# Gain vector by TensorE, remainder rows in strided DMAs, and an earlier second k-by-v product in a fused attention and mixer kernel

## The chip, the cores and the metric

The kernel runs on one core of a Trainium2 chip. The metric is the device time of one execution in microseconds. Before the change the median of three runs was 773.2 us (772.67 to 773.29). Where a single execution is taken apart, the numbers come from the profiled one: 772.69 us, of which the profile's span covers 770.6 us from the first to the last recorded instruction. Times inside the kernel are given from the span's start.

## The reference, cut to what matters

Eight batches, eight heads, 576 tokens, 64 elements to a head. Attention has no softmax: per head it forms `k`-transposed times `v` over the 576 tokens, multiplies `q` with that, divides each row by its root mean square and multiplies by the gain vector `g_norm` (64 numbers, the same for every token and head). The result goes through a mixer over tokens and then one over channels.

```python
kv  = einsum('bhsd,bhse->bhde', k, v)
out = einsum('bhsd,bhde->bhse', q, kv)
x   = out / sqrt(mean(out*out, -1) + 1e-6) * g_norm      # (B,H,S,D) -> (B,S,512)
h   = maximum(x.transpose(0,2,1) @ w_tok1, 0) @ w_tok2   # tokens: 576 -> 256 -> 576
u   = x + h.transpose(0,2,1)
out = u + maximum(u @ w_ch1, 0) @ w_ch2                  # channels: 512 -> 1536 -> 512
```

The four weights arrive as 64-bit floats. The kernel fetches them as pairs of 32-bit words and turns them into 32-bit floats itself.

## The kernel before, in words

**Tiling.** A batch's 576 tokens are split in 512 and a remainder of 64 (`LO` and `HF`, line 61). `k` and `v` of one batch lie in a tile of 128 partitions by five slots by 512 columns (lines 107 and 108): slots 0 to 3 hold the first 512 tokens, four to a partition, and slot 4 holds the 64 remainder rows in partitions 0 to 63. The other half of slot 4 is zeroed once (line 1285). There are two such pairs of tiles, so batch b uses pair b % 2.

**Loading.** `load(b)` (line 140) issues four DMAs: the 1 MB body of `k`, its 128 KB remainder (64 rows of 2 KB, line 148), and the same for `v`. For batch 0 `k` goes through SP's queue and `v` through ACT's; afterwards all go through SP's. `load_q(b)` (line 150) fetches `q`, already transposed, as `qT`. At the start SP issues, in this order, `load(0)`'s k part, `qT` of batch 0, two blocks of the first token weight (`raw`), `load(1)`, `qT` of batch 1, two `q` remainders and the rest of that weight (lines 1275 to 1283). ACT issues `v` of batch 0 and then `g_sb` (line 1294): the 64 gains, copied into all 128 partitions by a DMA whose source repeats the same 256 bytes 128 times.

The framework gives the DMAs of SP and ACT eight completion semaphores in turn, in program order. A DMA that comes ninth waits, on its issuing engine, for the landing of the one that had its semaphore before.

**Steps and their order.** The order of the work is written out by hand as strings of step names (`start`, `middle`, `steady`, `last`), which `play` (line 1256) executes one after the other; each engine runs its own instructions in that order and waits only on data. In the first list the names mean:

- `jN`: N products of the identity with itself, whose result nobody reads (`keep_warm`, line 1333); they keep TensorE busy while data is on its way.
- `kvSH`, `eSH`: k by v for batch S of the pair, half H of the heads (40 matmuls on TensorE, line 371); eviction of the result from PSUM (line 385; by DVE for batch 0 of the first pair, by ACT for batch 1).
- `aCT`: `q` by kv for token group C, tile T (`attend_tile`, line 394); `g`, `q`, `t`, `m`, `r`, `i`, then `d` or `s`: gain times the product (line 451, the reader of `g_sb`), squares, sums, mean, root, inverse, and scaling of the rows by DVE or ACT.
- `hSTJ`: one term of the first token product, batch S, half T of the 256 outputs, token tile J (`tok1`, line 539). It needs x of tile J, that is attention's result, and the weight.
- `wNK`: step K of decoding weight block N. `lS`, `lqS`, `lrS`: the loads of the next pair.

So the first product with a token weight (`h000`) needs the whole chain batch 0's `k`, `v` and `qT`, kv, attention, statistics, scaling and a decoded weight. From then on TensorE has token products, k by v and attention of following batches to alternate between, later the channel products, in which it spends most of the time.

PSUM is used through three pools; the pool `h` of four banks (line 97) serves the products nobody reads, the token products and later the residual sums.

Of the kernel before, what the change touches and what calls it, by code (L numbers as in the profile page):

```python
# [11 lines left out]
F32 = mybir.dt.float32  # L12
# [8 lines left out]
def kernel(  # L21
# [32 lines left out]
    nc = tc.nc  # L54
    P = 128
    B, S, DM = k.shape
    D = g_norm.shape[0]
    H = DM // D
    DTOK = moe_w_tok1.shape[1]
    DCH = moe_w_ch1.shape[1]  # L60
    J, JJ, HF = 4, 5, 64
    LO = P * J
    assert D == 64 and DM == 512 and S == LO + HF and B % 2 == 0
    NC, NF, NTOK = DM // P, DCH // P, DTOK // P
# [13 lines left out]
    def pool(name, bufs, side="left", stack=ctx, **kw):  # L78
        return stack.enter_context(tc.tile_pool(name=name, bufs=bufs, side=side,
                                                reuse_waits="tile", **kw))  # L80
# [9 lines left out]
    inp = pool("inp", 1, "left", left)  # L90
# [5 lines left out]
    ps = {n: pool(f"ps_{n}", b, "left", psums, space=bass.MemoryType.PSUM)  # L96
          for n, b in (("o", 2), ("kv", 2), ("h", 4))}

    ident = inp.tile([P, P], F32, name="ident")
    g_sb = inp.tile([P, 1, D], F32, name="g_sb")  # L100
    w_tok1 = [tokw.tile([P, 2, DTOK], F32, name=f"w_tok1{i}") for i in range(J // 2)]
    w_tok1r = tokw.tile([P, DTOK], F32, name="w_tok1r")
    w_tok2 = tokw.tile([P, NTOK, S], F32, name="w_tok2")
# [10 lines left out]
    def do(f, *a, **kw):  # L114
        return lambda: f(*a, **kw)
# [4 lines left out]
    keep = tc.keep_in_program_order  # L120

    def dma(o, i, engine=nc.sync):
        keep(engine.dma_start(o, i))  # L123
# [7 lines left out]
    def copy(o, a):  # L131
        keep(nc.scalar.copy(o, a))  # L132

    def matmul(*a, **kw):
        keep(nc.tensor.matmul(*a, **kw))  # L135
# [4 lines left out]
    def load(b):  # L140

        if b >= B:
            return

        queues = (nc.sync, nc.sync if b else nc.scalar)
        for dst, t, e in zip((k_in[b % 2], v_in[b % 2]), (k, v), queues):
            dma(dst[:, :J], t[b, :LO].rearrange("(p j) e -> p j e", j=J), e)
            dma(dst[:HF, J], t[b, LO:], e)

    def load_q(b):  # L150
        if b < B:
# [107 lines left out]
    def t_sums(b):  # L259

        def step(o, x, y):
            return lambda: tensor_add(b(o), b(x), b(y), ALU.subtract)

        return [step(5, 7, 1), step(6, 3, 5), step(7, 3, 7), step(4, 2, 6)]
# [96 lines left out]
    def attention(pair, groups):  # L361
# [154 lines left out]
        for s in range(2):  # L516
            for h in range(2):
                steps |= {f"kv{s}{h}": do(kv, s, h), f"e{s}{h}": do(evict, s, h),
                          f"l{s}": do(load, 2 * pair + 2 + s)}
            steps |= {f"lq{s}": do(load_q, 2 * pair + 2 + s), f"lr{s}": do(load_q_rest, 2 * pair + 2 + s)}  # L520
# [75 lines left out]


    xg, xt, uT = {}, {}, {}
    Q = 32
    NQ = T // Q  # L600

    def units(g):
        return ((0,), (1, 2), (3, 4), (5, B), (6, 7))[g] if g < NG else (NU, NU)

    def fetch_x(g):
# [4 lines left out]
        else:  # L610
            xg[g] = late["xg"].tile([P, 2 * NQ, 2, Q], F32, name="xg")
            for b in range(NC):
                dma(xg[g][ds(b * Q, Q)].rearrange("p n l j -> p n (l j)"),
                    u_rows(units(g)[0])[:, ds(DH + b * HF, HF)].rearrange("(n i) e -> i n e", i=Q))

# [14 lines left out]
    def put_blocks(u, half, y):  # L630
        t = blocks_dram[u, half] = dram.tile([NC, Q, NC, 2 * P], F32, name=f"blocks{u}{half}")
        for a in range(NC):
            dma(t[:, :, a].rearrange("b i x -> i b x"),
                y[ds(a * Q, Q)].rearrange("p b o n t -> p b (o n t)"))

# [620 lines left out]
    def play(lines, after={}, **stages):  # L1256

        for name in " ".join(lines).split():  # L1260
            if name.isdigit():
                for _ in range(int(name)):
                    next(stages["rounding"], lambda: None)()
            elif name[0] == "-":
                stages["before"][name[1:]]()
            else:
                next(stages[s][name] for s in ("attention", "mixing", "more")
                     if name in stages.get(s, ()))()
# [4 lines left out]
    channel = ([get_ch1(c, f) for f in range(2) for c in range(NC)]  # L1273
               + [get_ch2(f) for f in range(NF // 2)])
    load(0)
    load_q(0)
    for block in tok1[:2]:
        block[0]()
    load(1)
    load_q(1)  # L1280
    load_q_rest(0)
# [5 lines left out]
    for t in zeroed:  # L1287
# [3 lines left out]
    keep(nc.vector.memset(root, 1.0))  # L1291
    keep(nc.scalar.activation(root, root, AF.Sqrt))
    make_identity(nc, ident)
    dma(g_sb, bass.AP(tensor=g_norm.tensor, offset=g_norm.offset,
                      ap=[[0, P], [0, 1], list(g_norm.ap[0])]), nc.scalar)

    start = [
        "j14 kv00 e00", "kv01 e01 l0", "a00 g00 q00", "a01 g01 q01 t00 t01 m0 w01",
        "a10 w02 r0 i0 w03 d00 w04 q10 w30 w40 lq0", "a11 q11 s01 g10 g11 w11 j10",
        "h000 h010 w12 w13 w14 t10 t11 m1 r1", "h001 h011", "kv10 e10", "kv11 e11 i1 d10 d11 l1", "h002", "a20 q20",  # L1300
        "a21 q21 g20 g21 t20 t21 m2", "h012 h003 r2", "a30 g30 i2 d20 q30", "a31 q31 s21 g31 t30", "h013 t31 m3",
        "a40 q40 r3 i3 d30 s31 g40 t40 m4 r4 w21 i4 d40 lr0 lr1"]
    middle = [
        "h100 h110 h101 h111 w31 w22 w23 w24", "kv00 e00 -lq1 w32 w33 w34",
# [21 lines left out]
    more = {f"w{n}{k}": f for n, b in enumerate(tok1 + tok2) for k, f in enumerate(b)}  # L1326
# [6 lines left out]
    def keep_warm(n):  # L1333

        o = ps["h"].tile([P, DM], F32, name="ps_j", tag="h")
        for _ in range(n):
            matmul(o[:, :P], lhsT=ident, rhs=ident, start=True, stop=True)

    more |= {f"j{n}": do(keep_warm, n) for n in (10, 14)}
    play(start, attention=attentions[0], mixing=mixings[0], more=more)  # L1340
    play(middle, attention=attentions[1], mixing=mixings[0], before=attentions[0],
         more=more, rounding=rounding)
    for n in range(1, B // 2 - 1):
        play(steady[n - 1], attention=attentions[n + 1], mixing=mixings[n], before=attentions[n] | {"u8": mixings[n - 1]["u8"]},
             more=more, rounding=rounding)
# [16 lines left out]
    more = {f"c{i}": f for i, f in enumerate(t_sums(lambda n: uT[0][:, SB[n]]))}  # L1362
# [98 lines left out]
```

## Time and profile before

| what | value |
|---|---|
| median of the runs | 773.2 us (772.67 to 773.29) |
| profiled execution, its span | 772.69 us, 770.6 us |
| TensorE (PE) busy | 760.8 us, 99% of the span |
| VectorE (DVE), ScalarE (ACT), GpSimd (POOL) busy | 642.8, 277.5, 112.3 us |
| granted TensorE clock over the span | 0.999 |
| busy time of TensorE between 20.96 and 60 us | 39.03 of 39.04 us |
| DMA rate between 0 and 20.96 us, and between 20.96 and 60 us | 312 and 326 GB/s |
| DMA packets under 512 bytes in the first 25 us, the 4-byte completion marks included | 412 of 2648 |
| `g_sb`, 32 KB on ACT's queue, from issue (1.85 us) to landing | 9.9 us |
| `qT` of batch 0, 1 MB on SP's queue, from issue (1.79 us) to landing | 11.9 us |

A busy engine is one with at least one instruction under way. The idle time in front of an instruction is put down to what ended last among the things it waited for. The chain that ended last is followed back from the last instruction, at each step to what released it. DMA durations run from issue to the last of the 16 completion marks, so they include the time that a transfer queues behind others.

### The profile page before, as it was taken

Reading aid. Unit: us, or ns where it says so; the run is one execution under the profiler, and the core shown is the slowest. Engines: PE = TensorE matmul, PEld = TensorE weight load, DVE = VectorE, ACT = ScalarE, POOL = GpSimd, SP = SyncE. Lnnn points to the kernel's source line nnn. Section 1 sums busy time; section 2 is a strip of 40 time slices with the busy share of each in tenths; the row PEclk is TensorE's granted clock in tenths of the full one; section 3 lists DMA queues with packets and bytes.
Section 4 is the critical chain, followed back from the end, with each engine's and each line's share of the span. In section 5 each row is a group of like instructions: output and inputs, shape, how many; then the busy total and the mean of one; then the engine's idle time right before and its main releaser. Section 6 shows DMA issues by size and latency. Waiting matters only on the chain.

```text
span 770.6 us, 12663 instructions
## 1 busy us (share of the span) xinstructions
PE 760.8 (99%) x4682; PEld 612.8 (80%) x4682; DVE 642.8 (83%) x945; ACT 277.5 (36%) x555; POOL 112.3 (15%) x124
## 2 busy tenths in 40 slices
PE   7999999999999999999999999999999999999998
PEld 6665555445888888888888888888888888888887
DVE  2877897997766779999979889987998996798996
ACT  2466575764210233521144242223352224325221
POOL 1002020113410000002240001042000218000204
PEclk9999999999999999999999999999999999999999
DMA  9999999599799786589898577999659879955679
GB/s 308 318 336 385 378 355 358 187 318 338 251 275 355 261 288 194 163 271 203 221 230 257 152 227 220 251 188 271 196 153 284 175 220 205 209 146 155 152 200 119
DMA packets 137819, 188.29 MB, mean 244 GB/s; under 512 B 48800, under 2 KB 95392, under 8 KB 135712
## 3 DMA queue, kind: packets, MB, share of 16 engines
q1 hardware_dynamic: 101744, 167.54, 68.9%
q0 software_dynamic: 34816, 18.36, 15.9%
q10 hardware_dynamic: 1200, 1.61, 0.6%
q8 instruction: 37, 0.61, 0.3%
q14 instruction: 22, 0.18, 0.1%
HBM read 138.31 MB, written 49.15 MB: 243 GB/s over the span
## 4 chain that ended last, share of the span: by engine, by line
PE 97%; DMA 2%; DVE 1%; SPq 0%; issue 0%; ACT 0%
PE ps_d L135 28%; PE ps_b L135 19%; PE ps_a L135 19%; PE ps_h L135 8%; PE ps_u L135 8%; PE ps_v L135 5%; PE ps_c L135 3%; PE ps_o L135 2%; PE ps_kv L135 2%; PE ps_w L135 2%; DMA qT<-in_q_dram 2%; PE ps_r L135 0%; SPq L123 0%; DVE x L451 0%; DVE ms L472 0%; DVE x L509 0%
## 5 line engine op out<-in xcount | busy, mean ns | idle before, releaser
L135 PE MATMUL ps_d<-ui,w 128*128 128x256 f32 x504 | 118.6, 379 | 0.0
L135 PEld LDWEIGHTS ps_d<-ui,w 128*128 128x128 f32 x504 | 95.8, 190 | 13.0
L132 ACT COPY ps_d<-ps_a 128x768 f32<-128x768 f32 (+1 forms) x56 | 32.0, 571 | 199.9 <-PE ps_a L135 196.8
L126 DVE TENSOR_TENSOR v<-v,v 128x1536 f32<-128x1536 f32 (+2 forms) x70 | 103.3, 1483 | 0.3
L135 PE MATMUL ps_b<-sv,w 128*128 128x256 f32 x324 | 78.9, 379 | 0.0
L135 PE MATMUL ps_a<-v,w 128*128 128x256 f32 x324 | 78.7, 379 | 0.0
L1205 POOL DMA_DIRECT2D out_dram<-us x24 | 26.8, 1832 | 291.8 <-ACT p L132 286.2
L135 PEld LDWEIGHTS ps_b<-sv,w 128*128 128x128 f32 x324 | 61.2, 190 | 8.9 <-issue 0.6
L135 PEld LDWEIGHTS ps_a<-v,w 128*128 128x128 f32 x324 | 61.6, 190 | 8.4
L135 PE MATMUL ps_u<-h,w_tok 128*128 128x512 f32 (+1 forms) x160 | 64.7, 599 | 0.0
L135 PE MATMUL ps_d<-v,w 128*128 128x256 f32 x258 | 62.7, 379 | 0.0
L129 ACT ACTIVATE v<-v 128x768 f32<-128x768 f32 (+1 forms) x54 | 42.7, 822 | 55.1 <-DVE v L126 53.5
L135 PE MATMUL ps_h<-x,w_tok 128*128 128x512 f32 x128 | 57.7, 600 | 0.3 <-DVE w_tok L188 0.3
L1205 POOL DMA_DIRECT2D out_dram<-r x40 | 41.3, 1925 | 102.0 <-ACT p L132 80.2
L135 PE MATMUL ps_d<-sv,w 128*128 128x256 f32 x228 | 55.4, 379 | 0.0
L135 PEld LDWEIGHTS ps_d<-v,w 128*128 128x128 f32 x258 | 48.9, 190 | 6.6
L135 PEld LDWEIGHTS ps_u<-h,w_tok 128*128 128x128 f32 (+1 forms) x160 | 25.6, 179 | 31.1 <-issue 26.7
L135 PEld LDWEIGHTS ps_d<-sv,w 128*128 128x128 f32 x228 | 43.3, 190 | 5.9
L135 PE MATMUL ps_a<-uT,w 128*128 128x256 f32 x192 | 46.7, 379 | 0.0
L135 PEld LDWEIGHTS ps_h<-x,w_tok 128*128 128x128 f32 x128 | 23.4, 190 | 27.2 <-issue 24.3
L135 PE MATMUL ps_b<-ui,w 128*128 128x256 f32 x168 | 40.8, 379 | 0.0
L135 PEld LDWEIGHTS ps_a<-uT,w 128*128 128x128 f32 x192 | 36.5, 190 | 5.0
(165 smaller groups left out, 1291.4 us busy)
## 6 DMA issues: line engine op xcount, KB each, us to landing
w<-parts SPq DMA_DIRECT2D x168, 384.0 KB, 3.8
w<-parts SPq DMA_DIRECT2D x56, 192.0 KB, 3.8
uT<-blocks SPq DMA_DIRECT2D x36, 256.0 KB, 5.6
k_in<-in_k_dram SPq DMA_DIRECT2D x8, 1024.0 KB, 13.3
qT<-in_q_dram SPq DMA_DIRECT2D x8, 1024.0 KB, 12.7
out_dram<-x POOLq DMA_DIRECT2D x16, 512.0 KB, 7.5
v_in<-in_v_dram SPq DMA_DIRECT2D x7, 1024.0 KB, 15.8
raw<-in_moe_w_ch_dram SPq DMA_DIRECT2D x8, 768.0 KB, 12.4
```

The costliest lines, as they stand in the source:

```text
L126: keep(engine.tensor_tensor(out=o, in0=a, in1=b, op=op))
L129: keep(nc.scalar.activation(o, a, AF.Relu))
L132: keep(nc.scalar.copy(o, a))
L135: keep(nc.tensor.matmul(*a, **kw))
L1205: keep(nc.gpsimd.dma_start(to, t()[ds(b * Q, Q), at].rearrange("p n l j -> p n (l j)"), accum_op=ALU.add))
```

## The change

Three things are changed, all at the start of the kernel or in `load`:

1. `g_norm` is loaded once, as one row of 256 bytes, and spread over the 128 partitions by a product with a row of ones on TensorE (new step `gs`, between `kv01` and its eviction), which ACT copies from PSUM to `g_sb`. The row of ones is set by GpSimd.
2. The 64 remainder rows of `k` and `v` are loaded by two DMAs of 32 rows each, in every batch. The rows of one DMA are taken eight apart (rows 0, 8, 16, 24, then 1, 9, ...), the same way for `k` and for `v`; since k by v sums over tokens, their order does not matter.
3. In the first list the second batch's k by v (`kv10`, `kv11`) stands ahead of the terms for token tile 1 (`h001`, `h011`), which are spread between the attention steps that follow; `h002`, `h003` move accordingly. The unread products become 12 and 8 instead of 14 and 10.

```diff
-    J, JJ, HF = 4, 5, 64
+    J, JJ, HF, Q = 4, 5, 64, 32
+    g_row, ones = (inp.tile([1, n], F32, name=name) for n, name in ((D, "g_row"), (P, "ones")))
...
             dma(dst[:, :J], t[b, :LO].rearrange("(p j) e -> p j e", j=J), e)
-            dma(dst[:HF, J], t[b, LO:], e)
+            for n in range(0, HF, Q):
+                dma(dst[n:n + Q, J], t[b, LO + n:LO + n + Q].rearrange("(r e) d -> e r d", e=8), e)
...
-    dma(g_sb, bass.AP(tensor=g_norm.tensor, offset=g_norm.offset,
-                      ap=[[0, P], [0, 1], list(g_norm.ap[0])]), nc.scalar)
+    keep(nc.gpsimd.memset(ones, 1.0))
+    dma(g_row, bass.AP(tensor=g_norm.tensor, offset=g_norm.offset, ap=[[0, 1], list(g_norm.ap[0])]), nc.scalar)
+
+    def spread_g():
+
+        o = ps["h"].tile([P, DM], F32, name="ps_g", tag="h")
+        matmul(o[:, :D], lhsT=ones, rhs=g_row, start=True, stop=True)
+        copy(g_sb[:, 0], o[:, :D])
...
-        "j14 kv00 e00", "kv01 e01 l0", "a00 g00 q00", "a01 g01 q01 t00 t01 m0 w01",
-        "a10 w02 r0 i0 w03 d00 w04 q10 w30 w40 lq0", "a11 q11 s01 g10 g11 w11 j10",
-        "h000 h010 w12 w13 w14 t10 t11 m1 r1", "h001 h011", "kv10 e10", "kv11 e11 i1 d10 d11 l1", "h002", "a20 q20",
-        "a21 q21 g20 g21 t20 t21 m2", "h012 h003 r2", "a30 g30 i2 d20 q30", "a31 q31 s21 g31 t30", "h013 t31 m3",
+        "j12 kv00 e00", "kv01 gs e01 l0", "a00 g00 q00", "a01 g01 q01 t00 t01 m0 w01",
+        "a10 w02 r0 i0 w03 d00 w04 q10 w30 w40 lq0", "a11 q11 s01 g10 g11 w11 j8",
+        "h000 h010 w12 w13 w14 t10 t11 m1 r1", "kv10 e10", "kv11 e11 i1 d10 d11 l1", "h001", "a20 q20", "h011",
+        "a21 q21 g20 g21 t20 t21 m2", "h002 h012 r2", "a30 g30 i2 d20 q30", "a31 q31 s21 g31 t30",
+        "h003 h013 t31 m3",
```

In the order that the build gives each engine, DVE's instructions are the same as before. TensorE has the spreading product and the moved terms, ACT one copy more, GpSimd one memset more, and SP and ACT one DMA more for each `k` and each `v`. The semaphores rotate accordingly: the two `raw` blocks of the first token weight, which waited for nothing before, now wait for the bodies of `k` and `v` of batch 0 to land, and the second half of `v`'s remainder rows of batch 1 for the row of `g_norm`.

## The prediction

> **What bounds the kernel now.** I read first the page's chain of work that ended last, by engine.
>
> ```profile
> PE 97%; DMA 2%; DVE 1%; SPq 0%; issue 0%; ACT 0%
> ```
>
> TensorE is the bound; the 2% of DMA can only be where TensorE has nothing to do yet. Next the same chain in order of time, for the first 27 us: start, length, what.
>
> ```profile
> 1.79 11.89 DMA qT<-in_q_dram
> 13.69 0.14 issue
> 13.82 2.04 PE ps_o L135 x16
> 15.88 0.70 DVE x L451
> ...
> 20.31 0.61 DVE w_tok L188
> 20.92 0.04 issue
> 20.96 3.70 PE ps_h L135 x8
> 24.66 2.34 PE ps_kv L135 x69
> ```
>
> The end of the kernel hangs on the landing of batch 0's `qT` at 13.69. From `a00` (13.82) a chain of small steps, one engine after the other, takes 7.14 us to the first token product `h000` at 20.96. From there TensorE is the chain. The stages (length, then busy time and count of PE, PEld, DVE, ACT, POOL, clock, DMA share, GB/s) say whether it ever waits again:
>
> ```profile
> 20.96:60.00 39.04, 39.03 (x474) 23.70 (x475) 28.42 (x64) 20.62 (x55) 0.90 (x1) 1.00 1.05 326
> ```
>
> It does not: 39.03 of 39.04 us. So a gain is to be had only ahead of 20.96, and shifts all that follows, unless a transfer comes too late for the shifted work. Then the DMA rate, by the same view:
>
> ```profile
> 5.00:7.00 2.00, 2.00 (x11) 2.00 (x11) 0.00 (x0) 0.00 (x0) 0.00 (x0) 1.00 1.03 438
> ...
> 7.50:8.50 1.00, 1.00 (x7) 1.00 (x6) 0.00 (x0) 0.00 (x0) 0.00 (x0) 1.00 1.06 250
> 8.50:9.50 1.00, 0.97 (x16) 0.81 (x17) 0.00 (x0) 0.00 (x0) 0.00 (x0) 1.00 1.07 173
> 9.50:10.50 1.00, 0.38 (x13) 0.24 (x9) 0.00 (x0) 0.00 (x0) 0.00 (x0) 1.00 0.72 163
> 10.50:11.50 1.00, 0.88 (x30) 0.88 (x32) 0.00 (x0) 0.00 (x0) 0.00 (x0) 1.00 0.90 332
> 11.50:12.50 1.00, 1.00 (x42) 1.00 (x38) 0.42 (x1) 0.00 (x0) 0.00 (x0) 1.00 1.04 403
> ```
>
> The rate is 438 while the bodies of `k` and `v` move, 403 while `qT` moves alone, and 163 to 250 between, though the engines count as busy. In that trough the two remainders of 64 rows and the 128 copies of g go by. The packets say the same: the DMA view, asked for 7.5 to 10, has 176 on SP's queue that take 67.1% of 16 engines, 152 ns each; for 10.5 to 12, 259 that take 93.6%, 87 ns each. Both are 2 KB rows but for a few. The third dip, 244 GB/s from 18 to 19 us, has a remainder in it (`k` of batch 1) and no g; so the remainders cost by themselves.
>
> **The trough (edits 1 and 2).** From 7.5 to 10.5 pass 250 + 173 + 163 = 586 KB. At 403 GB/s that is 1.45 us instead of 3.0: 1.55 lost. The next microsecond loses 0.18. If all goes, `qT` lands 1.73 us earlier, at 11.96; if nothing goes, 0. At the fastest row, 438, all that moves from 7.5 to 13.1 (586 + 332 + 403 and 0.6 us at 408, together 1566 KB) needs 3.6 us, and `qT` would come 2.0 earlier. So the unknown is bounded by 0 and 2.0, and below 0 by a rival. I take the row of the same transfer without company, 403, hence 1.73.
>
> `a00` also needs batch 0's kv. The timeline shows how it stands:
>
> ```profile
> 9.20 0.69 PE L135 MATMUL ps_kv<-v_in,k_in 128*64 128x64 f32 x16
> ...
> 10.62 2.09 PE L135 MATMUL ps_kv<-v_in,k_in 128*64 128x64 f32 x64 [0.73 <-DMA v_in<-in_v_dram]
> ...
> 12.75 0.42 DVE L389 COPY kvp<-ps_kv 128x256 f32<-128x256 f32 x1 [0.74 <-PE ps_kv L135]
> ```
>
> The remainders land at 10.6, TensorE waits 0.73 us for them, and from there to the end of the second eviction (12.75 + 0.42 = 13.17) pass 2.55 us. Up to 9.5 the trough has lost 0.95 us (423 KB in 2.0), up to 10.5 1.55; I let the remainders land 1.1 us earlier, at 9.5. Then kv is evicted at 12.07. `a00`, whose third product needs the second eviction, starts at 12.2 with `qT` at 12.0: both causes meet there, which is why I count **1.6 us** of the 1.73. The chain of 7.14 us behind it has no transfer in it but the first `raw` block, which ACT takes at 17.10; it moves behind `qT`, 1.3 us of data later, to 13.4, and is wanted at 15.5. `h000` then starts at 19.36.
>
> A rule against the row. The row: 2 KB packets take 152 ns while the 64-row remainders pass, 87 without them. The Trainium skill, "DMA: Bandwidth & Descriptors", section "Why a DMA increments its semaphore by 16 and not by 1", says that a DMA runs on the largest number of engines up to 16 that divides the slowest dimension of both sides: 16 for 64 rows by 64, but 8 for 32 by 8, as the change has it. The rules for kernel authors there speak against that: use all 16 engines, and join small transfers. By the rule eight engines carry 16 rows each instead of 8, and at 87 ns that is 0.7 us more ahead of `qT`, which would leave 0.9 of the 1.6. "SBUF — State Buffer", section "Door 1", has 64 partitions reach 8 of 16 ports, so that 16 engines meet in pairs at a port; by that the double load is there today. The dip at 18 us agrees, but no row here names a port; I keep 1.6.
>
> **What the edits add.** The spreading product stands between `kv01` and `a00` on TensorE: two passes, between 0.06 us (29 ns each in kv: 64 in 2.09 us less the tail of the last) and 0.24 us (120 ns each, the 128x128 products of `j10`: 20 in 2.40 us), inside the wait for the eviction (0.42 us and more). Its row of g is queued behind `v`'s remainder on ACT's queue and lands with it, near 9.6; if it came after 12.2, `a00`, queued behind it on TensorE, would wait as long. ACT's copy (0.27 us by the 128x128 copy) must be ready at the first gain, 1.17 us after `a00` starts; ACT has nothing else there (12.4 us idle before its first square). GpSimd's memset (0.1 to 0.2 us by its others) comes after the identity, on which nobody else waits. SP and ACT issue one DMA more per load, 0.35 to 0.56 us; `qT`'s issue slides from 1.79 to 2.35, with bodies in the queue until 7.5. The two `raw` blocks, issued at 2.63 and 3.20 today, wait for the bodies to land and go out near 9; `qT`'s 1 MB covers this until 12. Were that cover gone they would start 1 us late, the slack of `raw` being 2. SP is 0% of the chain, and later loads land with over 1 us to spare (the remainder of batch 2's `v`, issued at 28.09, lands at 38.0; its products start at 39.2). So nothing there.
>
> Two unread products fewer: 28 took 5.83 us, 208 ns each, the last at 112; four fewer end it at 8.7 instead of 9.15. The granted clock reads 1.00 throughout, yet 20 later ones took 2.40 us, 120 each, so something speeds up near 8.4, and 12 products still reach past it. If not, kv would run slower, up to 2 us on TensorE; I hold it at nothing. Eight instead of ten end 0.45 us earlier inside the wait for `h000`.
>
> **The earlier second k by v (edit 3).** Work is the same; two more changes between token terms and attention cost 0.1 us together (0.06 at the first of `a20` today). Data is what matters. Today `kv10` starts at 24.6, behind four terms. Batch 1's `v` lands at 24.4 (issue 10.59 and 13.8 us), its remainder at 25.1 (10.98 and 14.1); TensorE loses 0.16 us there. After the change two terms (1.83 us) stand ahead: `kv10` starts at 19.36 + 1.83 = 21.2 and wants the remainder at 21.45. From `qT`'s landing to this remainder 3.41 MB move (two `raw` of 524 KB, two bodies, two remainders), in 11.4 us today, 299 GB/s; at 403 it is 8.5 us, at 438 7.8. So the remainder lands at 12.0 + 8.5 = 20.5; with the trace's own pace at 23.4. One 16 KB instruction packet in this stretch (1.2 us of one engine's time) holds up a sixteenth. I take 21.4, nearer to 403, as the remainders lose their dips. Then no wait: **-1.6 - 0.16 + 0.1 = -1.66 us**, 771.0 on the profiled execution's 772.69 and, since that stands 0.5 under the median, **771.5** against 773.2.
>
> Let L be that landing. When it binds, TensorE's shift is no longer set by `a00`: work behind `kv10` starts as today at L = 23.1 (24.6 - 1.83 for the two terms, + 0.26 for the products that don't need the remainder, + 0.16 lost today, - 0.1 for the changes), so the time changes by L - 23.1.
>
> **The rivals.**
> - *As forecast*, L up to 21.45: 771.5 (770.7 to 772.0). For: the trough, and a full TensorE behind. Against: two causes meet at 12.2.
> - *The second batch comes a little late*: the instruction packet hits a loaded engine, L = 22.3: -0.8, 772.4 (772.0 to 773.2). For: 20.5 to 23.4 is the honest span.
> - *Slower, one wait in place of another*: the remainders cost as much on fewer engines (each dip stays), L stays near 25.1, and the moved `kv10` waits for it with two token terms behind it that could have run: 25.1 - 23.1 = +2.0, 775.2. It decides from L = 23.1 on; over 0.2% from 24.7. For: half the engines, eight semaphores that now cover fewer bytes. Against: the trough exists only with 64-row remainders.
> - *The change doesn't do what it says*: the DMA is split as before, the trough loses only g's share, and gain and wait cancel: within 0.5 of 773.2.
>
> **Chances.** Forecast 0.60, of which three quarters lie below 771.65; a little late 0.20; slower 0.17; no effect 0.03. About 0.2%, 1.55 us, is what a measurement of this kernel can tell from no change. Faster 0.45; same 0.15 + 0.20 + 0.03 = 0.38; slower 0.17. The range goes from 770.7 (2.0 at 438 GB/s, and the runs' 0.5) to 773.3, and leaves out the slower case and the rim of the first.
>
> **What would show it.** Right: the 163 to 250 GB/s stretch is gone or halved; `qT` lands near 12, `a00` starts near 12.2, `h000` near 19.4; no 2 KB packets at 150 ns; `kv10` near 21.2 without a wait for `v_in`. Wrong: `qT` near 13.5; a wait of over 0.5 us in front of or in `kv10`; `a00` behind the spreading product; token products that wait for `raw`.

## The result and the profile after

| | before | after | ratio (95%) |
|---|---|---|---|
| median of ten runs each, side by side | 773.38 us | 771.43 us | 0.9971 (0.9961 to 0.9981) |
| the same kernels again, on another occasion | 773.05 us | 771.38 us | 0.9982 (0.9973 to 0.9991) |
| profiled execution, its span | 772.69, 770.6 us | 771.12, 769.3 us | |

The change makes the kernel faster: by 2.2 us (1.5 to 3.0) by the first ratio, by 1.4 us (0.7 to 2.1) by the second. The forecast was 771.5.

First the chain that ended last in the kernel after, in order of time (start, length, what). Before, this stretch began with `qT` and went on at 13.82 with `a00`.

```profile
0.75 7.97 DMA v_in<-in_v_dram
...
11.65 9.89 DMA v_in<-in_v_dram
21.54 0.14 issue
21.67 2.55 PE ps_kv L136 x80
24.23 1.06 PE ps_h L136 x2
25.28 1.09 PE ps_o L136 x8
```

`qT`, attention and the first token products have left the chain. What decides now is the body of batch 1's `v`, issued at 11.65 and landed at 21.54, and `kv10` behind it. TensorE's timeline (start, length, work, idle time ahead and what ended it) shows the steps to that point:

```profile
8.81 0.69 PE L136 MATMUL ps_kv<-v_in,k_in 128*64 128x64 f32 x16 [0.85 <-DMA v_in<-in_v_dram]
9.82 2.09 PE L136 MATMUL ps_kv<-v_in,k_in 128*64 128x64 f32 x64 [0.32 <-DMA v_in<-in_v_dram]
11.83 0.43 PE L136 MATMUL ps_g<-g_row,ones 1*128 1x64 f32 x2
12.19 2.05 PE L136 MATMUL ps_o<-kvp,qT 128*128 128x128 f32 x16
...
19.35 1.99 PE L136 MATMUL ps_h<-x,w_tok 128*128 128x512 f32 x4 [0.68 <-DVE w_tok L190]
21.67 2.55 PE L136 MATMUL ps_kv<-v_in,k_in 128*64 128x64 f32 x80 [0.34 <-DMA v_in<-in_v_dram]
```

`a00` starts at 12.19 and `h000` at 19.35, both 1.6 us earlier than before; the spreading product fits in the gap ahead of `a00`. In front of `kv10` TensorE now waits 0.34 us. The rates (the last two columns: DMA share, GB/s):

```profile
7.50:8.50 1.00, 0.46 (x5) 0.27 (x3) 0.00 (x0) 0.00 (x0) 0.00 (x0) 1.00 0.97 377
8.50:9.50 1.00, 0.69 (x16) 0.58 (x16) 0.00 (x0) 0.00 (x0) 0.00 (x0) 1.00 1.05 406
9.50:10.50 1.00, 0.68 (x23) 0.71 (x25) 0.00 (x0) 0.00 (x0) 0.00 (x0) 1.00 1.10 410
10.50:11.50 1.00, 1.00 (x42) 1.00 (x39) 0.42 (x1) 0.00 (x0) 0.00 (x0) 1.00 0.94 266
11.50:12.50 1.00, 1.00 (x18) 0.87 (x14) 0.42 (x1) 0.20 (x1) 0.00 (x0) 1.00 1.06 332
12.50:13.50 1.00, 1.00 (x11) 1.00 (x10) 0.04 (x1) 0.01 (x1) 0.00 (x0) 1.00 0.97 317
13.50:21.50 8.00, 6.57 (x43) 4.88 (x41) 7.51 (x18) 6.56 (x17) 0.00 (x0) 1.00 1.02 405
21.67:60.00 38.33, 38.33 (x488) 23.38 (x492) 27.36 (x64) 18.87 (x51) 1.46 (x2) 1.00 1.02 367
```

The old trough is gone: 1193 KB pass from 7.5 to 10.5 where 586 did. A new, shallower dip (266 to 332) lies behind it. From 21.67 to 60 TensorE is busy throughout, so that all of the difference was made by about 25 us. The first product with the remaining token weight (`w_tok1r`), a mark with the same steps in front of it in every kernel here (but for the unread products and the spreading), starts at 45.44 before and 44.19 after: 1.25 us, and the span is 1.3 shorter. Before's line and after's:

```profile
45.44 1.99 PE L135 MATMUL ps_h<-x,w_tok1r 64*128 64x512 f32 x8
44.19 1.99 PE L136 MATMUL ps_h<-x,w_tok1r 64*128 64x512 f32 x8
```

**How far such numbers carry.** Two executions with the same loads, before and `e4_order_only`, start `a00` at 13.82 and 14.30: single traces differ by half a microsecond there. And the time is not the span: by medians over all runs, 2.15 us of before's time lies outside the span, 1.78 of after's, 2.2 and 2.8 of one and the same other kernel (`e3_old_order`, run twice). By spans alone the change gains 1.3 (769.6 against 770.9) on the second occasion. So mechanisms are read below from marks in the trace, and verdicts from ratios. The spans of all runs are a third witness (e5, for one, is 1.0 us longer than before by them, at a ratio near 1): against before on the same occasion their medians stand at -0.1 us for e1, -1.5 for e2, -1.6 for e3 (-1.8 when run again), +1.5 for e4, +1.0 for e5, 0.0 for e6, -0.8 for e7, -0.4 for e8, -0.15 for e9 and -1.1 for e10.

### The profile page after: what moved, and what is told of

It is laid out like the page before. It is cut to its first block, busy times and chain, and to the rows that moved or that the text cites. A ratio compares the mean times of both kernels' runs of the same rounds, so it can differ in the third digit from the quotient of the medians.

```text
span 769.3 us, 12678 instructions
## 1 busy us (share of the span) xinstructions
PE 759.4 (99%) x4676; PEld 612.3 (80%) x4676; DVE 642.5 (84%) x945; ACT 277.4 (36%) x556; POOL 112.3 (15%) x125
## 4 chain that ended last, share of the span: by engine, by line
PE 97%; DMA 2%; SPq 0%; issue 0%; DVE 0%
PE ps_d L136 28%; PE ps_b L136 19%; PE ps_a L136 19%; PE ps_u L136 8%; PE ps_h L136 8%; PE ps_v L136 5%; PE ps_c L136 3%; DMA v_in<-in_v_dram 2%; PE ps_kv L136 2%; PE ps_o L136 2%; PE ps_w L136 2%; SPq L124 0%; PE ps_r L136 0%; DVE xs L127 0%
```

## The experiments

The prediction counts the trough as one sum. The expectations hold besides that in the trough the 64-row remainders cost most, g's 128 copies the rest, and that each edit gives back its part; the new order costs little, since the loads land sooner. The rivals: one of the two edits does all of it; the order takes back some of the gain. Letters in the expectations stand for theories that are told apart there: A that two engines write to the same few partitions at once and hold each other up, F that it is the place of g's copies, beside the remainders, that counts.

All results together. The last three columns are from the profiled execution: start of `a00`, of `kv10`, and of the product with `w_tok1r`. The medians come from four occasions, on which before had 773.38 us (after), 773.25 (e1 to e4), 773.56 (e5 to e8) and 773.05 (the others), so rows are compared by their ratios.

| kernel | median, us | ratio to before (95%) | a00 | kv10 | w_tok1r |
|---|---|---|---|---|---|
| before (profiled) | | | 13.82 | 24.60 | 45.44 |
| after | 771.43 | 0.9971 (0.9961 to 0.9981) | 12.19 | 21.67 | 44.19 |
| `after_again` | 771.38 | 0.9982 (0.9973 to 0.9991) | 12.34 | 21.52 | 44.06 |
| `e1_rows_only` | 773.77 | 1.0006 (0.9997 to 1.0014) | 14.22 | 25.00 | 45.73 |
| `e2_g_only` | 771.75 | 0.9979 (0.9970 to 0.9988) | 12.68 | 23.46 | 44.32 |
| `e3_old_order` | 771.74 | 0.9978 (0.9969 to 0.9988) | 12.26 | 23.06 | 43.79 |
| `e3_again` | 771.86 | 0.9983 (0.9974 to 0.9992) | 12.16 | 22.94 | 43.68 |
| `e4_order_only` | 774.69 | 1.0018 (1.0009 to 1.0027) | 14.30 | 24.62 | 47.35 |
| `e5_contiguous` | 773.77 | 1.0004 (0.9995 to 1.0013) | 13.26 | 23.87 | 46.79 |
| `e6_one_of_64` | 773.01 | 0.9997 (0.9987 to 1.0007) | 13.76 | 23.18 | 46.28 |
| `e7_h001_first` | 771.99 | 0.9980 (0.9971 to 0.9989) | 12.23 | 22.46 | 45.88 |
| `e8_g_from_rows` | 773.77 | 1.0004 (0.9995 to 1.0013) | 13.56 | 24.54 | 45.69 |
| `e9_g_behind_q` | 772.87 | 0.9998 (0.9988 to 1.0007) | 13.43 | 24.51 | 45.70 |
| `e10_rows_g_behind_q` | 771.81 | 0.9985 (0.9977 to 0.9994) | 12.23 | 23.00 | 43.73 |

### The parts by themselves

`e1_rows_only` is before with the second edit alone:

```diff
-            dma(dst[:HF, J], t[b, LO:], e)
+            for n in range(0, HF, Q):
+                dma(dst[n:n + Q, J], t[b, LO + n:LO + n + Q].rearrange("(r e) d -> e r d", e=8), e)
```

> The kernel before with the strided remainder DMAs alone; g still comes by 128 copies, the order and the unread products are those of before. My theory (the 64-row remainders make most of the trough, g the rest, and nothing else bounds the start): the 163 to 250 GB/s stretch shrinks to a short dip, qT lands near 12.4, a00 starts near 12.5, h000 near 19.7; the second batch is wanted only near 23.3 and is there: -1.3 to -1.5 us on the trace. Rival (g's 128 copies of one address are the trough): qT stays near 13.4, a00 near 13.5, at most -0.4 us.

Measured: no gain; the interval of the ratio takes in 1. The rates of this kernel, DMA share and GB/s last, say why:

```profile
7.50:8.50 1.00, 1.00 (x11) 0.87 (x11) 0.00 (x0) 0.00 (x0) 0.00 (x0) 1.00 0.83 296
8.50:9.50 1.00, 0.66 (x17) 0.52 (x16) 0.00 (x0) 0.00 (x0) 0.00 (x0) 1.00 0.68 223
9.50:10.50 1.00, 0.57 (x19) 0.60 (x21) 0.00 (x0) 0.00 (x0) 0.00 (x0) 1.00 0.68 193
```

The trough is nearly as deep, but it is another one. Before, the engines were busy with slow packets in the first two of the three rows (share 1.06 and 1.07) and partly idle in the third (0.72). Here a 2 KB packet takes 84 to 121 ns (means of half a microsecond; before, 162 to 228 between 8.0 and 10.0), and the engines stand idle a third of the time (0.68) while g's 128 small packets go by. `qT` lands at 14.09. The slow packets went with the 64-row remainders, and another cause in the same three microseconds took their place. A later dip is the 64-row remainders' own: where the remainder of batch 1's `k` passes and g does not, the rate is 244 GB/s before, and here

```profile
18.00:19.00 1.00, 1.00 (x12) 1.00 (x11) 0.95 (x4) 1.00 (x4) 0.00 (x0) 1.00 1.06 426
```

`e2_g_only` is before with the first edit alone: `g_row`, `ones`, `spread_g` and the step `gs` behind `kv01`.

> The kernel before with the spread of g alone; 64-row remainder DMAs, order and unread products as before. My theory: the trough loses g's share only, a00 starts 0.3 to 0.6 us earlier (13.2 to 13.5), -0.3 to -0.5 us on the trace. Rival (g is the trough): a00 near 12.4, -1.3 us or more.

Measured: 1.6 us (0.9 to 2.3) faster, as much as the whole change. The theory's 0.3 to 0.5 us missed; the rival's 1.3 or more came. The rates:

```profile
7.50:8.50 1.00, 0.68 (x7) 0.48 (x5) 0.00 (x0) 0.00 (x0) 0.00 (x0) 1.00 1.02 303
8.50:9.50 1.00, 0.48 (x16) 0.52 (x16) 0.00 (x0) 0.00 (x0) 0.00 (x0) 1.00 1.08 201
9.50:10.50 1.00, 0.53 (x17) 0.40 (x15) 0.00 (x0) 0.00 (x0) 0.00 (x0) 1.00 1.00 354
```

Two of the three are still low, and the engines' share is 1.00 to 1.08, with 2 KB packets of 138 to 189 ns from 8 to 9.5. This is the remainders' own loss. It is over about 1 us sooner without g, and `qT` lands at 12.54.

`e3_old_order` is after with before's list of steps (and `gs` in it), so both edits of the loads without the new order.

> The changed kernel with the order of before (second k by v behind h001 and h011) and 14 and 10 unread products. My theory (the order costs a wait of 0.4 us for v of batch 1 and brings nothing): a00 near 12.2 and h000 near 19.35 as in the changed kernel, kv10 starts near 23.0 without a wait, and the later token products stand 0.3 to 0.5 us earlier than in the changed kernel: -1.6 to -1.8 us against before on the trace. Rival (the order is part of the gain, because attention of the second batch is late without it): a wait of TensorE for DVE or ACT between 25 and 37 us, and -1.0 us or less against before.

Measured: 1.7 us (0.9 to 2.4) faster, not to be told from after, nor from e2. On the trace it is ahead of after: the product with `w_tok1r` starts at 43.79 and, when run again, at 43.68, against 44.19 and 44.06.

`e4_order_only` is before with after's list of steps, and the unread products as before.

> The kernel before with the new order alone (all loads and unread products as before). My theory (shift = landing of what kv10 wants, less 23.1 us): h000 at 20.96, kv10 is wanted at 22.8 and waits for v of batch 1, whose body landed at 24.4 and whose remainder at 25.1 in the trace of before: TensorE loses 1.6 to 2.0 us there, +1.5 to +2.0 us. Rival (the order brings something by itself, in attention): +0.5 us or less.

Measured: 1.4 us (0.7 to 2.1) slower; the mark on the trace is 1.9 late. Its timeline at that place:

```profile
21.45 1.98 PE L135 MATMUL ps_h<-x,w_tok 128*128 128x512 f32 x4 [0.32 <-DVE w_tok L188]
24.62 2.75 PE L135 MATMUL ps_kv<-v_in,k_in 128*64 128x64 f32 x80 [1.19 <-DMA v_in<-in_v_dram]
```

Two token terms, then 1.19 us of waiting for the body of batch 1's `v`, which lands at 24.48 (its remainder at 25.14), while two terms that could have run stand behind `kv10`. The forecast's formula for this case, L - 23.1, gives +2.0 for a remainder at 25.14.

### Which form of the rows

`e5_contiguous` is after with 32 rows to a DMA, but in their order:

```diff
-                dma(dst[n:n + Q, J], t[b, LO + n:LO + n + Q].rearrange("(r e) d -> e r d", e=8), e)
+                dma(dst[n:n + Q, J], t[b, LO + n:LO + n + Q], e)
```

> The changed kernel with the remainders as two DMAs of 32 neighbouring rows instead of 32 rows taken eight apart. Theory A (what slows the remainders is that 16 engines meet in pairs at the same partitions' way into memory; the strided form puts a DMA on eight engines, which the 1 + 8 completion marks of a strided remainder show): all 16 marks come from engines again, 2 KB packets take 130 to 170 ns between 7.5 and 9, the dip to about 200 GB/s is back, a00 near 12.7 as with the spread of g alone. Theory B (two smaller DMAs do it, or no remainder form matters): packets at 84 ns, a00 near 12.2.

`e6_one_of_64` is after with one DMA of 64 rows, eight apart:

```diff
-            for n in range(0, HF, Q):
-                dma(dst[n:n + Q, J], t[b, LO + n:LO + n + Q].rearrange("(r e) d -> e r d", e=8), e)
+            dma(dst[:HF, J], t[b, LO:].rearrange("(r e) d -> e r d", e=8), e)
```

> The changed kernel with the remainder as one DMA of 64 rows taken eight apart (row e of each group of eight, so eight engines with eight neighbouring partitions each). Theory A (pairs at the same partitions' way in): engine e then writes partitions 8e to 8e+7, and e and e+4 still meet, so packets above 84 ns remain, 100 to 170. Theory B (the number of engines or the stride is what counts): 84 ns and a00 near 12.2, with one DMA issue and one semaphore less per load than in the changed kernel.

Both lose the gain. The first two rows of each, e5's first:

```profile
7.50:8.50 1.00, 1.00 (x7) 0.89 (x5) 0.00 (x0) 0.00 (x0) 0.00 (x0) 1.00 1.03 293
8.50:9.50 1.00, 0.21 (x5) 0.16 (x6) 0.00 (x0) 0.00 (x0) 0.00 (x0) 1.00 1.07 179
```

```profile
7.50:8.50 1.00, 0.55 (x5) 0.36 (x4) 0.00 (x0) 0.00 (x0) 0.00 (x0) 1.00 1.00 272
8.50:9.50 1.00, 0.28 (x9) 0.32 (x11) 0.00 (x0) 0.00 (x0) 0.00 (x0) 1.00 1.07 254
```

The engines are fully busy and move little: between 8.0 and 9.5 a 2 KB packet takes 144 to 225 ns in e5 and 130 to 163 in e6 (means of half a microsecond). In after it is 84 at the same time. The completion marks tell how many engines a remainder had: sixteen marks as data land in e5; in e6 and after one mark right behind the issue and eight at the landing, so eight engines. Eight engines alone are not enough (e6), nor are 32 rows (e5). If the rows are dealt out to the engines in order, engine e of eight fills partitions 4e to 4e+3 in after, and those 32 further on in the second DMA; in e6 it fills 8e to 8e+7; in e5 each of sixteen fills two, in before four. Thus only in after no two engines fill the same group of four, or groups 32 apart. That fits theory A, but the dealing out is assumed, and no row of the trace names what the engines meet at. The Trainium skill, "SBUF — State Buffer", section "Door 1", says that partitions in groups of four, and those 32 further on, lie behind one port. By that engines would share a port in e5 and e6 and not in after; the packet times of the three kernels agree.

The order of edit 3 makes these two look worse at the mark (46.79, 46.28), as L, the landing of batch 1's last remainder, is late again: the body of `v` lands at 23.74 in e5, and TensorE waits 1.47 us ahead of `kv10`. L itself is 24.41 in e5 and 23.89 in e6, and L - 23.1 gives +1.31 and +0.79; the marks are 1.35 and 0.84 late. So the formula of the forecast holds in three kernels in which L binds, e4, e5 and e6, and by time the loss of the gain in e5 and e6 is that of the rows and the order together.

### Whether another order is better

`e7_h001_first` is after with one token term, `h001`, back in front of `kv10`, which should cover the 0.34 us wait:

```diff
-        "h000 h010 w12 w13 w14 t10 t11 m1 r1", "kv10 e10", "kv11 e11 i1 d10 d11 l1", "h001", "a20 q20", "h011",
+        "h000 h010 w12 w13 w14 t10 t11 m1 r1", "h001", "kv10 e10", "kv11 e11 i1 d10 d11 l1", "a20 q20", "h011",
```

> The changed kernel with h001 ahead of the second batch's k by v. My theory (kv10 waited 0.4 us for v of batch 1 in the changed kernel, the only cost of the new order): h000 near 19.35, kv10 wanted near 22.1, after the landing at 21.5, no wait; later token products 0.3 to 0.5 us earlier than in the changed kernel, 771.0 to 771.2. Rival (whatever stands there, the wait moves to the next load, qT of batch 1 at a20, or to DVE): the wait before a20 grows to 0.4 us and the time is as with the changed kernel, 771.4.

Measured: 1.5 us (0.9 to 2.2) faster than before, not to be told from after. The wait was to be gone; in the profiled execution it moved and grew:

```profile
22.46 2.76 PE L136 MATMUL ps_kv<-v_in,k_in 128*64 128x64 f32 x80 [0.23 <-DMA v_in<-in_v_dram]
26.93 1.13 PE L136 MATMUL ps_o<-kvp,qT 128*128 128x128 f32 x8 [1.71 <-DMA qT<-in_q_dram]
```

Fifteen of the sixteen marks of batch 1's `qT` are there by 25.08, the last comes at 26.80. One mark in sixteen is late already for the body of `k` (19.15, the others by 17.94), after a packet of 16 KB of the instruction queue that started at 15.04 and took 0.90 us. That it passed on the late engine fits, but the trace does not tell a packet's engine. In after the last mark of the same load came at 25.11, 0.47 us behind the one before it. How late that mark is differs from trace to trace, so this trace's 45.88 is not the kernel's typical one (its median span is 770.2; the profiled one has 771.0).

### What it is about g

`e8_g_from_rows` is before, but g's DMA reads 128 different rows in place of 128 times the same 256 bytes:

```diff
-    dma(g_sb, bass.AP(tensor=g_norm.tensor, offset=g_norm.offset,
-                      ap=[[0, P], [0, 1], list(g_norm.ap[0])]), nc.scalar)
+    dma(g_sb[:, 0], v[0, :P, :D], nc.scalar)
```

It leaves the gains out: each partition multiplies by 64 numbers of `v` instead.

> The kernel before, its gains read from 128 different rows of v (64 numbers of each) instead of 128 times from g_norm: the same number and size of packets, from 128 places. The output is not the reference's, since the gains are other numbers. Theory C (128 reads of the same 256 bytes hold up the engines): the stretch from 9.5 to 10.5 is as fast as without the copies (near 350 GB/s), a00 near 12.7. Theory D (128 small packets between large ones cost that wherever they come from): the trough stays, a00 between 13.8 and 14.3 as with the loads of before.

Measured: no difference from before (269, 184 and 179 GB/s in the trough, before 250, 173 and 163). So it is not that one address is read 128 times; 128 packets of 256 bytes cost as much from 128 places. The engines are not idle here, though: the share is 1.03, 1.13 and 1.01, where before has 0.72 in the third row.

`e9_g_behind_q` is before with g's DMA, unchanged, right behind `load_q(0)` on SP's queue, so that its copies pass behind `qT`. `e10_rows_g_behind_q` is the same with the strided remainders of e1.

```diff
     load_q(0)
+    dma(g_sb, bass.AP(tensor=g_norm.tensor, offset=g_norm.offset,
+                      ap=[[0, P], [0, 1], list(g_norm.ap[0])]))
```

> The kernel before with g still in 128 copies, but issued on SP's queue behind qT instead of on ACT's beside it; 64-row remainders, order as before. Theory F (the small packets cost because they come between the large ones of the other queue, at the same time as the remainders): the stretch is as with the spread of g alone, qT lands near 12.5 and a00 starts near 12.7; the copies pass behind qT, ahead of raw, which has the slack; -1.1 us on the trace, as with the spread by TensorE. Rival (128 packets cost the same wherever they stand): g lands past 13.5 and the first gain, wanted near 13.9, or the first decode of raw, wanted near 16, comes late; no gain.

> The strided remainder DMAs, and g in 128 copies behind qT on SP's queue; order and unread products of before, no spread by TensorE. Theory F: the trough is gone as in the changed kernel (no stretch under 330 GB/s before 10), a00 near 12.3, g there at 13.4, so the spread by TensorE can be had for the price of a moved line: the trace as the changed kernel with the order of before, -1.6 us. Rival: as with the strided rows alone, a00 near 14, no gain.

Measured: e9 gains nothing that can be told from none, e10 gains 1.2 us (0.5 to 1.8). In e9 the trough stays without any of g's copies in it, and the dip at 18 us stays as well:

```profile
7.50:8.50 1.00, 1.00 (x7) 1.00 (x6) 0.00 (x0) 0.00 (x0) 0.00 (x0) 1.00 1.05 279
8.50:9.50 1.00, 1.00 (x6) 0.85 (x5) 0.00 (x0) 0.00 (x0) 0.00 (x0) 1.00 1.12 184
9.50:10.50 1.00, 0.73 (x17) 0.58 (x16) 0.00 (x0) 0.00 (x0) 0.00 (x0) 1.00 0.99 195
...
18.00:19.00 1.00, 1.00 (x12) 1.00 (x11) 0.89 (x6) 1.00 (x3) 0.00 (x0) 1.00 1.15 258
```

The 64-row remainders alone can make all of it, and F falls for g alone. In e10 it is gone, and engines are idle later:

```profile
8.50:9.50 1.00, 1.00 (x21) 0.85 (x19) 0.00 (x0) 0.00 (x0) 0.00 (x0) 1.00 1.05 406
9.50:10.50 1.00, 0.66 (x23) 0.58 (x21) 0.00 (x0) 0.00 (x0) 0.00 (x0) 1.00 1.07 398
...
11.50:12.50 1.00, 0.80 (x21) 0.69 (x17) 0.42 (x1) 0.00 (x0) 0.00 (x0) 1.00 0.70 176
```

At 11.5 to 12.5 the share is 0.70 at 176 GB/s, much as in e1, now behind `qT`, where only the `raw` blocks follow, which have time. Not all of that is shown to be g's: after, e3 and e7 dip behind `qT` without its copies, though less far in that row (326 to 348 GB/s). And in e9, where the same 128 copies pass behind `qT`, the engines stay busy (share 1.07 and 1.05, 375 and 369 GB/s from 11.5 to 13.5). So with the strided rows g's copies go with idle engines, in e9 they do not, and no run tells why. The spreading by TensorE is one way to get g out of the trough; with strided rows another place in the queue gains as much as can be told by time (0.9985, e3 on the same occasion 0.9983).

Four kernels alike but for the form of the rows and g's place in the queues make a square: before, e1 with strided rows (1.0006), e9 with g behind `qT` (0.9998), and e10 with both (0.9985). Neither change alone gains anything, both together do.

### The same kernels again

> The changed kernel once more, beside the two that follow. Theory E (whether the second batch's v is late depends on where the 16 KB instruction packet of the first 20 us falls: on an engine with remainder rows it delays the last of 16 marks by 1 to 1.5 us, on one without it costs nothing): a00 near 12.2 and h000 near 19.35 again, the wait before kv10 anywhere from 0.3 to 1.5 us, so the first product with the remaining token weight anywhere from 44.1 to 45.9 us. Rival (0.4 us is the price of the order as such): 44.2 again.

> The changed kernel with the order and the unread products of before, once more, for the same comparison in the same job. Theory E: a00 and h000 as in the changed kernel, no wait or a short one before kv10, 43.8 to 44.6 for the first product with the remaining token weight; the time within 0.1% of the changed kernel's, on the better side. Rival (the new order is what made the changed kernel faster): 0.1% or more slower than the changed kernel.

Measured: 0.9982 and 0.9983. TensorE is idle ahead of `kv10` for 0.03 us in this execution of after (0.34 in the first), below the 0.3 to 1.5 of theory E. Neither order can be told from the other by time; by the mark on the trace the old order is 0.4 us ahead both times (43.79 against 44.19, 43.68 against 44.06), and by the medians of the spans 0.5 (769.1 against 769.6).

## Why the prediction was right, and where it was not

- **What bounds the kernel**: right. All of the difference arises ahead of about 25 us, and TensorE is full from there on.
- **The trough in sum**: right. `qT` was to land at 11.96 and landed at 12.02; the remainders of `v` at 9.5, and 9.57; the row of g at 9.6, and 9.77; `a00` at 12.2, and 12.19; `h000` at 19.36, and 19.35. The 2 KB packets of 150 ns are gone: 84.
- **What the trough is made of**: wrong. The step that failed is "the trough exists only with 64-row remainders": e1 has none and a trough of 296, 223 and 193 GB/s. The sign stood in the prediction's own row 9.50:10.50, read as "though the engines count as busy" while its share is 0.72. "So the remainders cost by themselves" holds: e9 has the trough without g, and the dip at 18 us, 244 before, is 412 GB/s in after, 426 in e1 and 258 in e9. But the expectations then took the two losses as shares that add up, and both forecasts for the parts missed (e1 -1.3 to -1.5 us, measured none; e2 -0.3 to -0.5, measured -1.6). There are two causes in the same three microseconds, slow packets beside the 64-row remainders and a loss that goes with g's copies, and either can fill them: e9 has only the first, e1 only the second, and `a00` starts at 13.43 and 14.22. Only with both gone is it near 12.2 each time (12.16 to 12.34 in after, e3, e7, e10 and the repeats).
- What stays open: e2 and e9 both have 64-row remainders and none of g's copies beside them, yet `qT` lands at 12.54 in the one and 13.30 in the other. Most of the difference is there when the body of batch 0's `v` lands, at 8.93 and 9.46, before any of g has landed in either; its remainder lands at 10.12 and 10.88. Two executions with the same loads, before and e4, are 0.6 us apart at that body as well (9.11, 9.73), but the times of ten or eleven runs differ too (0.9979 and 0.9998). The two were measured on different chips, each against before on its own, and no run puts them side by side. So why taking g out of the trough gains in e2 and not in e9 is not settled.
- **`kv10` without a wait**: wrong by 0.4 us. The step that failed is L, "I take 21.4, nearer to 403". Batch 1's remainder landed at 21.85, its body at 21.54: from `qT`'s landing the 3.41 MB took 9.83 us, 347 GB/s, where 9.4 us were taken. Two things show in the trace. From `qT`'s landing to 13.5 the rate was 332 and 317, and only then 405, an estimated loss of 0.3 us against 403. And a landing is that of the last engine: seven of the eight marks of the last remainder come from 20.86 to 21.28, the eighth at 21.85. The issue of `v` also moved from 10.59 to 11.65, behind the two `raw` blocks and one remainder more; no run shows that this cost anything, since it lies ahead of `qT`'s landing, with `raw` and the body of `k` still to move. With the measured 21.85 the formula L - 23.1 gives -1.25, which is what the mark shows.
- **The sum**: forecast -1.66, on the trace -1.25: -1.61 at `h000`, +0.41 at `kv10`, -0.16 for the loss of before that is gone, +0.12 for a wait at `a20`, whose `qT` lands at 25.11. On the profiled execution that would be 771.4 instead of the 771.0 forecast; it measured 771.12. That the median still hit 771.5 is luck: 0.4 us less lies outside the span than before, which nothing in the prediction stands for.
- **Costed at nothing**: the spreading product (0.43 us) lay inside the wait for the eviction, as said; `raw` was issued at 8.74 and 9.15 (forecast near 9) and landed at 13.65 and 15.48 without a product waiting for it. The speeding up of TensorE came at 6.9 us instead of 8.4 and kv ran at full speed; `kv00` waited 0.85 us for its body, which costs nothing, since the remainder is later. The step from 14 and 10 unread products to 12 and 8 has no run of its own; e3 keeps 14 and 10 and is as fast.
- **The rivals**: the slower one named a real mechanism, as e4 shows with +1.4 us and a 1.19 us wait. It did not decide here because L fell from 25.1 to 21.85, below its point of 23.1. But the third edit brings nothing either: with the same loads, e3 is at least as fast. The whole gain is that of the loads, and by time the spreading of g alone (e2) already has all of it.
- **The rule against the row**: the Trainium skill, "DMA: Bandwidth & Descriptors", section "Why a DMA increments its semaphore by 16 and not by 1", was right on the number of engines: eight marks at the landing for 32 by 8. Its advice for authors, to use all 16, was the ground for a loss of 0.7 us on eight engines, which did not come: the remainders landed at 9.57, as forecast without it. The fairest pair is e9 and e10, alike but for the rows, sixteen engines against eight: `a00` at 13.43 and 12.23, ratios 0.9998 and 0.9985. So the measurement decides against the advice here. By time it does not do so everywhere: e2, with sixteen, is as fast as after.

## What to carry to other kernels

A stretch with a low rate can have two causes that hide each other: take away each alone and both together (before, e1, e9, e10) before judging either. The engines' share beside the rate can show that there is a second one (1.07, then 0.72 in the prediction's rows), but it does not name it: e7 has 0.86 at 215 GB/s without a copy of g, and e8 has the copies with no idle engine. And before work is moved ahead of a load, work out when the load lands after the change, not before it: 25.1 us made the new order cost 1.4 us by itself, 21.85 made it nearly free.

## What the runs showed of the hardware that was not expected

- Rows loaded by half the engines can land sooner than by all: 2 KB packets took 84 ns in after, on eight engines, and 144 to 225 in e5, on sixteen, and the remainders of batch 0's `v` landed at 9.57 and 10.63.
- 128 packets of 256 bytes on a second queue beside strided rows went with idle engines (share 0.68 in e1, against 1.05 and 1.10 in after without them). From 128 addresses they cost as much as from one (e8, 64-row remainders), there without idle engines.
- The 64-row remainders slow what passes with them on the same queue: from 18 to 19 us the 8 KB packets took 555 ns in before and 309 to 317 in after and e1.
- With strided remainders and no g beside them the rate dips behind the old trough, at 10.5 to 13.5 us: to 215 to 348 GB/s in after, e3 and e7. It is another kind of dip: the median 2 KB packet still takes 84 or 85 ns, and single ones take up to 1.0 or 1.2 us. There is none in e2, e5 and e6 (377 to 393). In after, eight of the sixteen engines have finished `qT` by 11.22 and the others from 11.66 on, so that half of them are a transfer ahead. Whether this is the cause wasn't tried.
- TensorE's unread products, which start at 3.34 or 3.35 us, change from 213 to 112 ns apart at 6.2 us (e4), 6.4 (e2), 6.9 (after, e3), 8.2 (e10, and after when run again), 8.4 (before), and not at all in e9 (last start 9.27), while the granted clock reads 1.00 throughout. The Trainium skill, "TensorE: Matmul & The Clock Gate", section "Part 1: The HAM clock gate", has the array at half its clock until a free-running window of activity has passed, so that the moment varies, by 500 ns either way. The spacing here agrees, the spread is larger, some 3 us, and the clock column does not show the change.
